# Two heads' scores of summed queries: 128 queries stationary, a PSUM bank for each head, and a new table of priorities

## The chip, the cores and the metric

The kernel runs on one core of one Trainium2 chip. The metric is the device time of one execution in microseconds (us). The kernel before took 773.06 us, the median of three runs that lie between 772.82 and 773.5 us. Instructions run on five engines: TensorE (PE in the profile), VectorE (DVE), ScalarE (ACT), GpSimd (POOL) and SyncE (SP), which here issues the DMAs.

## The reference

Three stages follow each other, all in float32.

- Attention over 4 batches, 8 heads, 576 positions of width 64, in two parts that are added. In the first, q, k and v are averaged over groups of four positions, which leaves 144 positions; softmax attention over these 144 gives an output that is repeated four times. In the second each position attends to the positions less than four away.
- A gated layer on 2304 tokens of width 512: `xk` and `xr` mix each token with the one before it, `k = relu(xk @ w_k)`, `v = k*k @ w_v` (1024 wide inside), `r = sigmoid(xr @ w_r)`, result `r * v`.
- A layer norm and a second pair of products, `x + relu(xn @ w_ch1) @ w_ch2`, 2048 wide inside.

```python
s = scale * np.matmul(qq, kk.transpose(0, 1, 3, 2))      # here 144 x 144 for each batch and head
s = s - np.max(s, axis=-1, keepdims=True)
a = np.exp(s)
a = a / (np.sum(a, axis=-1, keepdims=True) + 1e-09)
return np.matmul(a, vv)
```

## The kernel before, in words

The attention is cut into 16 units of one batch and two heads (`attention(n, ...)`). Head 0 lies on partitions 0 to 63, head 1 on 64 to 127. A unit loads q, k and v by DMA, brings q and k into a layout with the width on the partitions (`tq`, on TensorE, or a transpose on VectorE), sums groups of four (`qd`, `kd`), and computes the local scores (`sc`, two tiles of 48 small products and a mask) and the scores of the sums (`ds`). The softmax of `ds` takes a maximum (`mxd`, VectorE), a scaling by a small factor, and three exponentials on ScalarE (`pd`, one for each of three tiles of 144 columns). Then come transposes of `pd` (`tp`), the product with the summed v (`up`), the local product with v (`pv`), and the sum of the two into `xT`. With 144 queries in a head and 128 partitions, the kernel before computes three tiles: queries 0 to 63, 64 to 127 and 80 to 143 of both heads, each head on 64 output partitions. All three lie in one PSUM bank.

The second stage goes over 6 chunks of 384 tokens. For each chunk there are `psr` (36 products of 512 columns, `moe_r`), `psk` (96 of 384 columns, `moe_k`) and `psv` (72 of 512 columns, `accumulate`). Each product of two float32 matrices is written as three products of a high and a low part (`mm3`), which is why the names end in h and l. Weights come as raw words of 64 bits per element, are turned into float32 by ScalarE (lines 395 and 397) and VectorE (402 and 406), and are split into high and low parts (375, 376, 420). The third stage has `psh` and `pso` in the same manner.

What sets the order: every operation is first put on a list with an engine or a choice of engines, an estimated cost and a priority (`Plan.add`). `Plan.order` then goes through a model of the engines: among the operations that could start first, the one with the lowest priority number is taken, buffers are handed out in the order of their first use's priority, and short operations on TensorE (`thin`) may be kept together. The priorities come from the table `PRM` of some 150 numbers, so that any change of the table moves instructions on all engines. Each engine runs its own list in order; a waiting instruction holds all behind it. Where the model has TensorE idle, up to the moment at which the accumulators of the first chunk are handed out, the order is filled with products that nothing uses, line 433 (`warm`):

```python
if until.t is None:
    for _ in range(int((o.at - free) / fill_cost)):
        fill()
```

The PSUM has 8 banks: three for `pv0` to `pv2`, two in the ring `pk` (for `psr`, `psk`, `psh`) and three in the ring `pa`, from which all attention tiles of batches 1 to 3 are taken (line 445, `psa`). In batch 0, tiles are taken from a longer ring over all three groups.

Of the kernel before, what the change touches and what calls it, by code (L numbers as in the profile page):

```python
# [19 lines left out]
P = 128  # L20
# [4 lines left out]
    thin=89.915, t0=-16.294, t1=-9.875, t2=6.158, t3=7.667, t4=48.796, t5=19.99, t6=6.382, t7=-23.592, t8=-0.47,  # L25
    t9=-5.238, t10=-2.702, t11=0.12, t12=5.747, t13=-8.176, t14=-15.681, t15=-4.758, m0=2, m1=1, m2=0, m3=3, m4=1,
    m5=0, m6=0, m7=2, m8=3, m9=0, m10=0, m11=0, m12=0, m13=0, m14=0, m15=0, g0=0, g1=0, g2=0, g3=0, g4=0, g5=0, g6=0,
    g7=0, g8=0, g9=0, g10=0, g11=0, g12=0, g13=0, g14=0, g15=0, h0=1, h1=1, h2=1, h3=1, h4=0, h5=0, h6=0, h7=0, h8=0,
    h9=0, h10=0, h11=0, h12=0, h13=0, h14=0, h15=0, dve=0.27, pool=0, ta=-14.632, u0=4.274, tl=26.492, tm=4222.228,
    ld=33.163, ldv=76.41, mu=-14.605, wr=-0.059, wrs=-31.134, wka=-33.615, wkas=7.94, wkb=12.502, wkbs=-165.286,  # L30
    wv=103.601, wvs=2.875, wld=0.932, d0=235.165, d1=108.349, d2=260.708, d3=463.399, d4=581.694, d5=82886.056,
    a1=13.725, a1s=43.62, a1l=52.7, a2=-1.632, a2s=26.831, a2l=56.61, a3=54.215, a3s=40.382, a3l=96.628, xr=-60.685,
    xrs=16.307, xk=22.171, xks=1.12, xrn=9, xrns=1.512, xkn=-4.695, xkns=17.37, w2a=10.707, w2as=1.55, w2=7.281,
    w2s=34.846, wc=10.079, wcs=106.739, m2q=8, sld=-6.173, x1=3, wcg=-39.001, p0l=11.872, p0=2.352, p0s=3.263,
    p0n=7.723, dp=684.729, ra0=-8.097, ra1=-1.757, ra2=3.642, ra3=4.616, ra4=-5.44, ra5=0, rb0=0.342, rb1=19.209,
    rb2=16.653, rb3=33.463, rb4=10.116, rb5=0, rx0=-2.918, rx1=-13.421, rx2=8.601, rx3=12.062, rx4=-2.926, rx5=5.409,
    ne=12, we=52.842, wes=25.704, wel=6.378,
# [23 lines left out]
class Plan:  # L61
# [61 lines left out]
    def order(self):  # L123
# [17 lines left out]
        for k in sorted(range(nb), key=lambda k: first[k], reverse=True):  # L141
            turn[tag[k]].append(k)
# [123 lines left out]
def attn_moe_kernel(  # L266
# [186 lines left out]
    def attention(n, T0, TL):  # L453
# [194 lines left out]
        ds_ = psa(b, "ds")  # L648

        def dscore():  # L650
            if first:
                warm_up(2)
            for t, q0 in enumerate((0, 64, SD - 64)):
                for hp in range(2):
                    nc.tensor.matmul(
                        ds_()[64 * hp:64 * hp + 64, SD * t:SD * t + SD],
                        qd()[64 * hp:64 * hp + 64, q0:q0 + 64],
                        kd()[64 * hp:64 * hp + 64, :],
                        start=True, stop=True,
                    )  # L660
# [642 lines left out]
```

## Time and profile before

| | before |
|---|---|
| median of 3 runs | 773.06 us |
| the profiled execution | 771.95 us |
| its span, first to last instruction | 770.2 us |
| mean granted TensorE clock | 0.999 |
| TensorE busy | 753.6 us (98%) |
| VectorE busy | 524.6 us (68%) |
| ScalarE busy | 398.2 us (52%) |
| GpSimd busy | 63.8 us (8%) |

The profiled execution is one run with a profiler on; its span is 1.75 us shorter than its own time. "Busy" is the share in which at least one instruction was running on an engine. Matmuls overlap each other on TensorE, so that the step from one start to the next is the cost of a product, not its duration. One float32 product of the kernel in attention shows as two records (12 records of `ds` are 6 instructions).

### The profile page before, as it was taken

The page shows a single profiled execution, that of the slowest core. Times are in us where ns is not written, and L with a number is a line of the kernel's source. Part 1 is how long each engine was busy: PE and PEld are TensorE (multiplying, and loading weights), DVE is VectorE, ACT ScalarE, POOL GpSimd, SP SyncE. Part 2 cuts the span into 40 slices and gives each one's busy share as a digit, 9 for nine tenths or more (in the row PEclk, how much of TensorE's full clock was granted, in tenths as well). Part 3 has the DMA queues.
Part 4 walks back from the last instruction along what each step waited for, and adds up shares of the span by engine and source line. Part 5 has one row for each costly group of instructions (what it writes and reads, how often), then busy time and mean ns, then how long its engine had stood idle before and what let it go on. Part 6 is the DMA issues. An engine that isn't in the chain of part 4 may idle for free.

```text
span 770.2 us, 15665 instructions
## 1 busy us (share of the span) xinstructions
PE 753.6 (98%) x5816; PEld 650.2 (84%) x5816; DVE 524.6 (68%) x1083; ACT 398.2 (52%) x916; POOL 63.8 (8%) x113
## 2 busy tenths in 40 slices
PE   9999999999999999999999999999999999999997
PEld 6878787788788798888888888889889899889886
DVE  6899999998985959878889763486543364333233
ACT  6889997987884847868835431221421131111110
POOL 3101122112100000000110000020000020000000
PEclk9999999999999999999999999999999999999999
DMA  8997596867768895964689894379853347443322
GB/s 190 208 192 180 180 180 124 182 170 144 207 159 267 251 323 171 290 217 135 141 281 289 208 258 121 112 246 305 183 150 115 112 121 258 138 120 113 123 69 82
DMA packets 202854, 140.88 MB, mean 183 GB/s; under 512 B 127120, under 2 KB 160028, under 8 KB 202780
## 3 DMA queue, kind: packets, MB, share of 16 engines
q1 hardware_dynamic: 202780, 139.90, 66.6%
q8 instruction: 46, 0.75, 0.4%
q14 instruction: 28, 0.23, 0.1%
HBM read 107.88 MB, written 31.98 MB: 182 GB/s over the span
## 4 chain that ended last, share of the span: by engine, by line
PE 77%; DVE 10%; DMA 6%; ACT 4%; issue 2%; POOL 0%; SPq 0%; DVEq 0%; POOLq 0%; ACTq 0%
PE pso L779 8%; PE pso L778 8%; PE pso L780 8%; PE psh L778 7%; PE psh L779 7%; PE psh L780 7%; PE psk L778 4%; PE psv L778 4%; PE psk L780 3%; PE psk L779 3%; PE psv L779 3%; PE psv L780 3%; DMA w<-in_moe_w_ch_dram 3%; PE warm L433 2%; DVE tmu L802 1%
## 5 line engine op out<-in xcount | busy, mean ns | idle before, releaser
L778 PE MATMUL psh<-xn,sa 128*128 128x384 f32 x336 | 114.0, 339 | 2.4 <-DVE c L1114 1.2
L779 PE MATMUL psh<-xn,sa 128*128 128x384 f32 x336 | 113.6, 338 | 0.0
L780 PE MATMUL psh<-xn,sa 128*128 128x384 f32 x336 | 113.3, 337 | 0.0
L778 PEld LDWEIGHTS psh<-xn,sa 128*128 128x128 f32 x336 | 63.1, 188 | 11.0 <-DVE c L1114 2.1
L779 PEld LDWEIGHTS psh<-xn,sa 128*128 128x128 f32 x336 | 63.1, 188 | 6.1 <-DVE xn L1051 0.2
L780 PEld LDWEIGHTS psh<-xn,sa 128*128 128x128 f32 x336 | 63.1, 188 | 0.0
L379 ACT ACTIVATE c22h<-t 128x384 fp32r<-128x384 f32 x24 | 12.6, 525 | 83.7 <-DVE t L1106 78.6
L395 ACT ACTIVATE wf<-w 128x512 f32<-128x512 f32 x48 | 32.3, 673 | 17.4 <-DMA w<-in_moe_w_ch_dram 9.2
L402 DVE SCALAR_TENSOR_TENSOR wf<-wf,w 128x512 uint32<-128x512 uint32 x48 | 32.9, 687 | 11.1 <-ACT w L397 10.6
L379 ACT ACTIVATE kr<-psk 128x384 f32<-128x384 f32 x46 | 22.4, 488 | 25.2 <-PE psk L780 21.2
L379 ACT ACTIVATE c11h<-psh 128x384 fp32r<-128x384 f32 x23 | 11.3, 491 | 45.8 <-PE psh L780 45.7
L397 ACT ACTIVATE w<-w 128x512 uint32<-128x512 uint8 x52 | 35.0, 672 | 0.0
L843 DVE TENSOR_TENSOR kl<-kr,kh 128x384 fp32r<-128x384 f32 x43 | 23.8, 553 | 14.6 <-ACT kr L842 14.3
L1083 DVE SCALAR_TENSOR_TENSOR c11l<-psh,c11h 128x384 fp32r<-128x384 f32 x24 | 13.3, 554 | 29.1 <-ACT c11h L379 29.1
L802 DVE SCALAR_TENSOR_TENSOR tmu<-xT,oms,tmu 128x384 f32<-128x384 f32 (+1 forms) x64 | 31.7, 512 | 1.8 <-ACT tmu L796 1.8
L406 DVE SCALAR_TENSOR_TENSOR wf<-w,wf 128x512 uint32<-128x512 uint32 x48 | 32.7, 680 | 0.3
L1106 DVE TENSOR_TENSOR t<-psh,t 128x384 f32<-128x384 f32 x24 | 13.3, 554 | 28.5 <-PE psh L780 28.4
L1097 DVE TENSOR_TENSOR u<-psh,u 128x384 f32<-128x384 f32 x24 | 13.3, 555 | 27.2 <-PE psh L780 27.1
L379 ACT ACTIVATE c12h<-c 128x384 fp32r<-128x384 f32 x24 | 12.6, 525 | 37.0 <-DVE c L1110 36.9
L379 ACT ACTIVATE c21h<-c 128x384 fp32r<-128x384 f32 x24 | 12.6, 523 | 34.6 <-DVE c L1114 34.6
L796 ACT ACTIVATE tmu<-xT,vecs 128x384 f32<-128x384 f32 (+1 forms) x51 | 26.8, 539 | 6.9 <-DVE xrl L806 4.0
L1103 DVE TENSOR_TENSOR t<-psh,u 128x384 f32<-128x384 f32 x24 | 13.2, 552 | 20.2 <-PE psh L780 20.1
(527 smaller groups left out, 2164.5 us busy)
## 6 DMA issues: line engine op xcount, KB each, us to landing
sa<-s_dram SPq DMA_DIRECT2D x168, 256.0 KB, 2.7
w<-in_moe_w_ch_dram SPq DMA_DIRECT2D x32, 512.0 KB, 6.2
s_dram<-s SPq DMA_DIRECT2D x56, 256.0 KB, 4.0
vw<-in_v_dram SPq DMA_DIRECT2D x62, 96.0 KB, 4.0
x_dram<-r SPq DMA_DIRECT2D x18, 256.0 KB, 3.4
x1t<-x_dram SPq DMA_DIRECT2D x6, 768.0 KB
z_dram<-x1t SPq DMA_DIRECT2D x18, 256.0 KB, 2.7
zb<-z_dram SPq DMA_DIRECT2D x96, 48.0 KB, 2.8
```

Source lines behind the costliest of these rows:

```text
L379: return [("ACT", c_act(n, True), lambda: nc.scalar.activation(dst(), src(), AF.Relu), False), ("DVE", c_dve(n), lambda: nc.vector.tensor_ ...
L395: add("ACT", c_act(512), prio, lambda: nc.scalar.activation(f(), w64().bitcast(F32)[:, :, 1], AF.Abs, scale=2.0 ** -112), r=[w64], w=[f])
L397: add("ACT", c_act(512), prio, lambda: nc.scalar.activation(w64()[:, :, 0], w64().bitcast(U8).rearrange("p a (b c) -> p a b c", c=4)[:, :, ...
L402: lambda: nc.vector.scalar_tensor_tensor(fu(), fu(), 3, w64()[:, :, 0], op0=ALU.logical_shift_left, op1=ALU.bitwise_or),
L406: lambda: nc.vector.scalar_tensor_tensor(fu(), w64()[:, :, 1], 0x80000000, fu(), op0=ALU.bitwise_and, op1=ALU.bitwise_or),
L433: nc.tensor.matmul(warm()[:, :304], identb, isumb, start=True, stop=True)
L778: nc.tensor.matmul(ps, lh, rh, start=start, stop=False, skip_group_check=more)
L779: nc.tensor.matmul(ps, lh, rl, start=False, stop=False, skip_group_check=more)
L780: nc.tensor.matmul(ps, ll, rh, start=False, stop=stop, skip_group_check=more)
L796: add([("ACT", c_act(n, ap=1), lambda t=t, o=o, n=n, cur=cur, kt=kt: nc.scalar.mul(t()[:, o:o + n], cur(), mu[:, kt:kt + 1]), False), ("DV ...
L802: lambda t=t, o=o, n=n, prv=prv, kt=kt: nc.vector.scalar_tensor_tensor(t()[:, o:o + n], prv(), om[:, kt:kt + 1], t()[:, o:o + n], op0=ALU. ...
L843: add(either(C, lambda e: e.tensor_tensor(kl(), kr(), kh().bitcast(F32), op=ALU.subtract)), 0, prio, None, r=[kr, kh], w=[kl])
```

## The change

The scores of the sums are laid out anew. For each head one product takes queries 0 to 127 as the stationary operand, with 64 rows (the width) and 128 output partitions, and each head writes a bank of its own. The last 64 queries (80 to 143) of both heads follow as before, in the second 144 columns of the first bank. So there are four products in place of six, two banks in place of one, and two maxima on VectorE (over 288 and over 144 columns) in place of one over 432. The three exponentials read the same three tiles of 144 columns, in another arrangement of queries, and the transposes of `pd` write to correspondingly other columns. The planner's cost of the group goes from 1.0 to 0.65. Buffers whose first use has the same priority are now ordered by number, and nearly all numbers of `PRM` are replaced (two lines are shown).

```diff
-    thin=89.915, t0=-16.294, t1=-9.875, t2=6.158, t3=7.667, t4=48.796, t5=19.99, t6=6.382, t7=-23.592, t8=-0.47,
+    thin=86.006, t0=-18.938, t1=-10.122, t2=5.262, t3=7.862, t4=41.79, t5=17.974, t6=-4.597, t7=-24.316, t8=4.432,
...
-        for k in sorted(range(nb), key=lambda k: first[k], reverse=True):
+        for k in sorted(range(nb), key=lambda k: (first[k], k), reverse=True):
...
-        ds_ = psa(b, "ds")
+        ds_ = [psa(b, "ds") for _ in range(2)]
...
-            for t, q0 in enumerate((0, 64, SD - 64)):
-                for hp in range(2):
-                    nc.tensor.matmul(
-                        ds_()[64 * hp:64 * hp + 64, SD * t:SD * t + SD],
-                        qd()[64 * hp:64 * hp + 64, q0:q0 + 64],
-                        kd()[64 * hp:64 * hp + 64, :],
-                        start=True, stop=True,
-                    )
-
-        add("PE", 1.0 + hold(2), pr(0.3), dscore, r=[qd, kd], w=[ds_] + held, thin=True)
-        dsv = lambda: ds_()[:, :3 * SD].rearrange("p (t c) -> p t c", c=SD)
+            for hp in range(2):
+                nc.tensor.matmul(ds_[hp]()[:, :SD], qd()[64 * hp:64 * hp + 64, :P], kd()[64 * hp:64 * hp + 64, :],
+                                 start=True, stop=True)
+            for hp in range(2):
+                nc.tensor.matmul(ds_[0]()[64 * hp:64 * hp + 64, SD:2 * SD], qd()[64 * hp:64 * hp + 64, SD - 64:],
+                                 kd()[64 * hp:64 * hp + 64, :], start=True, stop=True)
+
+        add("PE", 0.65 + hold(2), pr(0.3), dscore, r=[qd, kd], w=ds_ + held, thin=True)
+
+        dsv = lambda: [ds_[0]()[:, :SD], ds_[0]()[:, SD:2 * SD], ds_[1]()[:, :SD]]
...
-        add("DVE", c_dve(432), pr(0.35),
-            lambda: nc.vector.tensor_reduce(mxd()[:, 0:3], dsv(), axis=AX.X, op=ALU.max), r=[ds_], w=[mxd])
+        add("DVE", c_dve(288), pr(0.35),
+            lambda: nc.vector.tensor_reduce(mxd()[:, 0:2], ds_[0]()[:, :2 * SD].rearrange("p (t c) -> p t c", c=SD),
+                                            axis=AX.X, op=ALU.max), r=[ds_[0]], w=[(mxd, 0)])
+        add("DVE", c_dve(144), pr(0.35),
+            lambda: nc.vector.tensor_reduce(mxd()[:, 2:3], ds_[1]()[:, :SD], axis=AX.X, op=ALU.max),
+            r=[ds_[1]], w=[(mxd, 2)])
...
-                lambda t=t: nc.scalar.activation(pd()[:, t], dsv()[:, t], AF.Exp, bias=mxd()[:, t:t + 1],
+                lambda t=t: nc.scalar.activation(pd()[:, t], dsv()[t], AF.Exp, bias=mxd()[:, t:t + 1],
...
-                r=[ds_, mxd], w=[(pd, t), (stat, 12 + t)])
+                r=[ds_[t // 2], mxd], w=[(pd, t), (stat, 12 + t)])
...
-                for t, q0 in enumerate((0, 64, SD - 64)):
-                    nc.tensor.transpose(tpv()[:, :, q0:q0 + 64], pd()[:, t, HS * kt:HS * kt + HS], ident)
+                for t, to in enumerate((tpv()[:, 0, :P], tpv()[:, :, SD - 64:], tpv()[:, 1, :P])):
+                    nc.tensor.transpose(to, pd()[:, t, HS * kt:HS * kt + HS], ident)
```

How the order changes is shown at three places. The first is TensorE in the first chunk of the second stage, right behind the first `psr` products, where the first `psk` products of the chunk stand (`xkh` and `xkl` are the chunk's tokens, `wk00h` to `wk30l` the weights of four blocks of 128 rows). Before, a group of `ds`, a second tile of `psk`, and five of the seven fill products that stand behind the first `psr`:

```order
L780 MATMUL psk<-xkh,wk20l 128x384
L655 MATMUL ds<-kd,qd 64x144 x6
L778 MATMUL psk<-xkh,wk00h 128x384
...
L780 MATMUL psk<-xkh,wk20l 128x384
L433 LDWEIGHTS identb
L433 MATMUL warm<-isum,identb 128x304
...
L778 MATMUL psk<-xkh,wk30h 128x384
```

Now, the same engine at the first group of `ds` in this chunk:

```order
L782 MATMUL psk<-xkh,wk30h 128x384
L783 MATMUL psk<-xkl,wk30h 128x384
L784 MATMUL psk<-xkh,wk30l 128x384
L655 MATMUL ds<-kd,qd 128x144 x2
L658 MATMUL ds<-kd,qd 64x144 x2
L782 MATMUL psk<-xkh,wk00h 128x384
```

The first two tiles of `psk` now run over all four blocks of weights before `ds`, and all fill products stand ahead of the first `psr`. Over the whole program, fill products go from 135 to 152: those ahead of the first `psr` from 128 to 152, those behind it from 7 to none. Changes between the wide products (`psr`, `psk`, `psv`, `psh`, `pso`) and anything else go from 93 to 105. One of the tiles of local scores (25 products) moves from ahead of the first `psr` to behind it. The split of the last block of `w_r` (`wr0l`, line 420) stays the 104th entry of VectorE's list, and its load the eighth load of a weight block in SyncE's.

The second place is TensorE at the border between the first and the second chunk. Before (`psv` with `wv7h` is the last of eight steps of an accumulator; `psv_1501` and `psv_1526` are its second and third accumulator):

```order
L780 MATMUL psr<-wr3h,xrl 128x512
L778 MATMUL psv_1501<-wv7h,kh 128x512
L779 MATMUL psv_1501<-wv7l,kh 128x512
L780 MATMUL psv_1501<-wv7h,kl 128x512
L778 MATMUL psr<-wr0h,xrh 128x512
...
L707 MATMUL tp<-isum,pd 72x2x64 x6
L778 MATMUL psv_1526<-wv7h,kh 128x512
L779 MATMUL psv_1526<-wv7l,kh 128x512
L780 MATMUL psv_1526<-wv7h,kl 128x512
L655 MATMUL ds<-kd,qd 64x144 x6
L718 MATMUL up<-pdT,vd 64x144 x4
L778 MATMUL psk<-xkh,wk00h 128x384
```

Now (the second and third accumulators are `psv_1459` and `psv_1469`):

```order
L782 MATMUL psv_1459<-wv7h,kh 128x512
L783 MATMUL psv_1459<-wv7l,kh 128x512
L784 MATMUL psv_1459<-wv7h,kl 128x512
L722 MATMUL up<-pdT,vd 64x144 x4
L752 MATMUL pv<-PT,vw 64x96 x12
L558 MATMUL tq<-isum,kin 128x120 x6
L782 MATMUL psv_1469<-wv7h,kh 128x512
L783 MATMUL psv_1469<-wv7l,kh 128x512
L784 MATMUL psv_1469<-wv7h,kl 128x512
L558 MATMUL tq<-isum,qin 128x120 x4
L782 MATMUL psr<-wr0h,xrh 128x512
```

All three accumulators of the first chunk are finished ahead of the first `psr` of the second, where two of them used to end between and behind its `psr` products.

The third place is VectorE in the first unit. Before:

```order
L640 TENSOR_REDUCE mx<-sc 128x6
L643 TENSOR_TENSOR e<-sc,mx 128x192
L420 TENSOR_TENSOR wr2l<-wf,wr2h 128x512
L667 TENSOR_REDUCE mxd<-ds 128x3
L677 TENSOR_REDUCE stat<-e 128x12
```

Now:

```order
L640 TENSOR_REDUCE mx<-sc 128x6
L667 TENSOR_REDUCE mxd<-ds 128x2
L420 TENSOR_TENSOR wr2l<-wf,wr2h 128x512
L643 TENSOR_TENSOR e<-sc,mx 128x192
L670 TENSOR_REDUCE mxd<-ds 128x1
L681 TENSOR_REDUCE stat<-e 128x12
```

The one maximum has become two, with other work between them.

## Rows read from the trace of the kernel before

**Rows 1.** The page's head: span, and TensorE's busy time.

```profile
span 770.2 us, 15665 instructions
...
PE 753.6 (98%) x5816; PEld 650.2 (84%) x5816; DVE 524.6 (68%) x1083; ACT 398.2 (52%) x916; POOL 63.8 (8%) x113
```

**Rows 2.** Windows: stretch, its length, then each engine's busy time (instructions).

```profile
2.00:57.30 55.30, 52.98 (x963) 41.27 (x961) 45.83 (x106) 41.66 (x117) 8.28 (x30) 1.00 1.03 203
57.30:240.00 182.70, 179.39 (x2310) 147.12 (x2301) 164.08 (x359) 153.65 (x396) 30.45 (x56) 1.00 0.73 171
240.00:460.00 220.00, 214.72 (x1044) 187.69 (x1043) 176.76 (x356) 138.85 (x279) 12.38 (x11) 1.00 0.80 238
```

**Rows 3.** Groups on TensorE: busy us, mean ns of one record, idle before.

```profile
L433 PE MATMUL warm<-isum,identb 128*128 128x304 bf16 x135 | 22.8, 308 | 2.0 <-DVE identb L326 1.8 <-issue 0.2
...
L655 PE MATMUL ds<-kd,qd 64*64 64x144 f32 x192 | 15.2, 291 | 0.0
```

**Rows 4.** Timeline around one `ds`: start us, duration us, engine, line, tiles, records.

```profile
161.68 0.33 PE L779 MATMUL psk<-xkl,wk31h 128*128 128x384 f32 x1
...
161.85 0.34 PE L780 MATMUL psk<-xkh,wk31l 128*128 128x384 f32 x1
...
162.12 0.95 PE L655 MATMUL ds<-kd,qd 64*64 64x144 f32 x12
...
163.00 1.21 PE L748 MATMUL pv<-PT,vw 128*64 128x96 f32 x24
...
164.14 0.50 PE L778 MATMUL psv<-wv2h,kh 128*128 128x512 f32 x1
...
164.47 0.39 PE L779 MATMUL psv<-wv2l,kh 128*128 128x512 f32 x1
```

**Rows 5.** Timeline of TensorE: fill products, full-height products, one tile of local scores.

```profile
25.77 2.24 PE L433 MATMUL warm<-isum,identb 128*128 128x304 bf16 x16
27.85 0.82 PE L707 MATMUL tp<-isum,pd 128*72 128x128 f32 x6
28.50 1.47 PE L604 MATMUL vs<-vw,wsum 128*72 128x128 f32 x12
29.91 0.72 PE L748 MATMUL pv<-PT,vw 128*64 128x96 f32 x12
...
72.27 0.25 PE L623 MATMUL sc<-maskb,identb 128*128 128x192 bf16 x1
...
72.99 0.26 PE L623 MATMUL sc<-maskb,identb 128*128 128x192 bf16 x1
```

**Rows 6.** Timeline ahead of the first `psr`, on ScalarE, VectorE and TensorE.

```profile
52.33 0.67 ACT L395 ACTIVATE wf<-w 128x512 f32<-128x512 f32 x1 [1.11 <-DMA w<-in_moe_w_r_dram]
...
56.93 0.92 DVE L420 TENSOR_TENSOR wr0l<-wf,wr0h 128x512 fp32r<-128x512 f32 x1
...
57.31 0.49 PE L778 MATMUL psr<-wr0h,xrh 128*128 128x512 f32 x1
```

**Rows 7.** Timeline at the second chunk: a store, ScalarE, TensorE.

```profile
136.81 1.86 SPq L863 DMA_DIRECT2D x_dram<-r  x1
...
142.45 0.60 ACT L822 ACTIVATE r<-psr 128x512 f32<-128x512 f32 x1 [1.70 <-DMA x_dram<-r]
...
143.10 0.44 PE L778 MATMUL psk<-xkh,wk00h 128*128 128x384 f32 x1 [1.48 <-ACT r L822]
```

**Rows 8.** Groups on VectorE: maxima over 192 and over 432 columns.

```profile
L640 DVE TENSOR_REDUCE mx<-sc 128x6 f32<-128x192 f32 x32 | 10.9, 346 | 1.0 <-PE sc L629 0.7
...
L667 DVE TENSOR_REDUCE mxd<-ds 128x3 f32<-128x432 f32 x16 | 9.5, 596 | 0.5 <-PE ds L655 0.4
```

**Rows 9.** Waits of TensorE for a PSUM tile's reader: total, times, longest (us).

```profile
PE tq L561 <- ACT ups L371: 1.0, 1, 1.0
...
PE tp L707 <- DVE xT L762: 0.4, 1, 0.4
```

**Rows 10.** Timeline: the last exponential that reads the `ds` of rows 4.

```profile
166.03 0.36 ACT L673 ACTIVATE pd<-ds,mxd 128x144 f32<-128x144 f32 x1
```

More of the change, by code (lines that the diff above doesn't have):

```diff
@@ L24 @@
 PRM = dict(
-    thin=89.915, t0=-16.294, t1=-9.875, t2=6.158, t3=7.667, t4=48.796, t5=19.99, t6=6.382, t7=-23.592, t8=-0.47,
-    t9=-5.238, t10=-2.702, t11=0.12, t12=5.747, t13=-8.176, t14=-15.681, t15=-4.758, m0=2, m1=1, m2=0, m3=3, m4=1,
+    thin=86.006, t0=-18.938, t1=-10.122, t2=5.262, t3=7.862, t4=41.79, t5=17.974, t6=-4.597, t7=-24.316, t8=4.432,
+    t9=-1.734, t10=4.242, t11=2.521, t12=0.116, t13=-10.093, t14=-4.939, t15=0.537, m0=2, m1=1, m2=0, m3=3, m4=1,
     m5=0, m6=0, m7=2, m8=3, m9=0, m10=0, m11=0, m12=0, m13=0, m14=0, m15=0, g0=0, g1=0, g2=0, g3=0, g4=0, g5=0, g6=0,
@@ L28 @@
     g7=0, g8=0, g9=0, g10=0, g11=0, g12=0, g13=0, g14=0, g15=0, h0=1, h1=1, h2=1, h3=1, h4=0, h5=0, h6=0, h7=0, h8=0,
[L29 to L37, printed above, removed]
+    h9=0, h10=0, h11=0, h12=0, h13=0, h14=0, h15=0, dve=0.286, pool=0, ta=13.998, u0=1.184, tl=23.071, tm=131.241,
@@ new lines @@
+    ld=38.056, ldv=129.431, mu=10.979, wr=6.876, wrs=-20.584, wka=-4.642, wkas=-2.051, wkb=14.259, wkbs=-32.139,
+    wv=113.112, wvs=3.386, wld=4.014, d0=203.946, d1=108.617, d2=425.731, d3=739.989, d4=1681.185, d5=5849569.365,
+    a1=5.837, a1s=41.207, a1l=48.778, a2=-1.89, a2s=26.385, a2l=49.833, a3=56.847, a3s=46.97, a3l=104.3, xr=-89.593,
+    xrs=22.848, xk=1.227, xks=5.399, xrn=9, xrns=0.867, xkn=-5.275, xkns=23.433, w2a=8.19, w2as=3.025, w2=-5.375,
+    w2s=47.665, wc=11.401, wcs=179.004, m2q=8, sld=-6.112, x1=3, wcg=-11.958, p0l=19.184, p0=-9.347, p0s=5.577,
@@ L38 @@
+    p0n=8.772, dp=762.448, ra0=9.241, ra1=-0.583, ra2=-20.548, ra3=-2.197, ra4=-6.884, ra5=0, rb0=-6.748, rb1=26.087,
+    rb2=3.111, rb3=48.319, rb4=-10.85, rb5=0, rx0=-4.413, rx1=-34.086, rx2=-4.413, rx3=-1.916, rx4=-4.961, rx5=2.524,
+    ne=12, we=98.705, wes=20.88, wel=3.677,
 )
```

## The prediction

> **What bounds the kernel now.** I read the page's head first: TensorE is busy for 753.6 of 770.2 us [rows 1], so the end can move only by what TensorE has to do and by the 16.6 us in which it does nothing. The windows say where those lie: 2.3 us between 2 and 57.3 us (the start, up to the first `psr`), 3.3 us between 57.3 and 240 us (attention of the later batches mixed with the second stage), 5.3 us between 240 and 460 us; the rest is before the first and behind the last product [rows 2]. From 460 us on there is none. VectorE is not the bound over the whole, but it has only 18.6 us to spare in the 182.7 us of the second window. TensorE's busy time is not all useful: 135 fill products hold 22.8 us, most of them at the start, and the `ds` groups 15.2 us [rows 3]. The profiled execution took 771.95 us, 1.1 us under the median of 773.06. Every term below is a difference against the profiled execution, and I put it on the median.
>
> **The products of `ds`.** One group before goes from 162.12 to 163.00 us: 0.88 us for 12 records [rows 4]. `psk` in front of it takes 0.27 us to the next start where its neighbour takes 0.17, and `psv` behind the thin group 0.33 to the next start [rows 4]: entering such a group costs TensorE about 0.1 us, and leaving it as much. The 12 records start in pairs, two heads at a time: 12 x 0.073. That they run together follows from products over the full height: 12 records of 128 columns take from 28.50 to 29.91 us, 0.117 each, and `ds` has 144 columns at 0.073 [rows 5, 4]. Now 8 records stand in place of 12. If the two heads with 128 output columns each run side by side as before, the group takes 8 x 0.073 = 0.59 us. The two kinds of product, 64 by 128 and 64 by 64, now stand next to each other, which the trace of before does not show; a switch of shape inside the group may cost what entering one does, 0.1 us, so 0.69 at the other end. I take 0.64, a saving of 0.24 us for a group. If they run one after the other, the first four records cost between 0.117 each and, scaled from 128 to 144 columns, 0.13; with 0.29 for the other four and 0.1 for the switch the group takes 0.86 to 0.91, so between 0.02 saved and 0.03 lost.
>
> The Trainium skill has a rule on this: TensorEngine Tiling (Array Packing), section Tiling Modes, says that changing the tiling mode, not just the tile, drains the engine. It speaks against the change, since a group now holds two modes. The 0.1 us on entering a group in rows 4 agrees with it in kind. By that rule alone a group takes 0.69 us, 16 groups save 0.8 us less than with my 0.64.
>
> **The fill products.** 16 of them take from 25.77 to 27.85 us, 0.13 each [rows 5]. Ahead of the first `psr` there are 24 more, +3.1 us; four `ds` groups there save 1.0; one tile of local scores leaves (72.27 to 72.99 us, 0.72 each [rows 5]). TensorE's own list ahead of the first `psr` is so 1.4 us longer. But TensorE stood idle for 2.3 us there [rows 2], waiting, and what the first `psr` needs last is the split of the last block of `w_r`: ScalarE, with all its list behind it, waits 1.1 us for the load, until 52.33, VectorE writes `wr0l` from 56.93, and `psr` starts at 57.31 [rows 6]. The order leaves that split and that load at the same place in their lists. So the fill takes the place of waiting. Bounds: 57.3 + 1.4 - 2.3 = 56.4 us if all waits vanish in it, 57.3 + 1.4 = 58.7 us if none does. I take 57.3, no change.
>
> **TensorE behind the first `psr`.** Seven fill products go: -0.9 us. The tile of local scores comes in: +0.7. Twelve groups of `ds` save 12 x 0.24 = 2.9. There are 12 more changes between wide products and others, at 0.1 us: +1.2. Sum -1.9 us (-2.5 with 0.59, -1.3 with 0.69, +0.8 with no saving). The transposes of `pd` keep their number and size, and I cost them at nothing, as only the columns that they write differ. Nothing hides them: all 96 lie on TensorE, so 0.01 us more or less for each would be 1 us.
>
> **The border of the chunks.** At 143.10 TensorE waits 1.48 us for ScalarE to empty a `psr` bank; ScalarE waits for a buffer `r`, and that for its store, issued at 136.81 and landed 5.6 us later [rows 7]. The store is late as the second accumulator of the first chunk ends among the `psr`. In the new order all accumulators end ahead of the `psr`, and 24 `psr` products with score tiles and a `ds` group stand between, some 8 us, against 0.7 for the multiplication, 5.6 for the store. I take the wait as gone: -1.5 us (bounds -1.5 and, if the loads ahead of the store on SP hold it longer, +1).
>
> **VectorE.** One maximum over 432 columns took 596 ns, one over 192 takes 346 [rows 8]: 1.04 ns a column and 146 ns fixed. 288 and 144 columns cost 446 + 296 = 742 ns, 0.15 more; 12 groups behind the first `psr` are 1.8 us more, against 18.6 us to spare [rows 2]. TensorE has other products to run meanwhile; if that cover is missing, all 1.8 us and the delay of other VectorE work come on top.
>
> **PSUM.** A `ds` group now holds two of the three banks of the ring, from its start at 162.12 to the last exponential at 166.03 [rows 4, 10], nearly 4 us in which scores, transposes, `up` and `pv` share one bank. TensorE waits for a reader of such tiles seldom now, 1.0 us at `tq` in the start and 0.4 at `tp` behind it [rows 9], the trace doesn't show it with two banks held. Bounds: 0, as the order puts `psk` and `psv`, which use other banks, between; and 0.4 us, the wait at `tp`, for each of the 12 units, 4.8 us. I take 1.0 us for PSUM and VectorE together, near the lower end, since the rows show so few waits.
>
> The Trainium skill says of it, TensorEngine Tiling (Array Packing), section Restrictions and Gotchas, that row tiling raises the pressure on PSUM because different row tiles must write to different banks. The second bank is that price; how long TensorE waits for it no row of before shows.
>
> **Sum.** 0 at the start, -1.9 behind it, -1.5 at the border, +1.0 for the new waits: -2.4 us, 773.06 - 2.4 = 770.7 us.
>
> **The rivals.**
> - *The start decides.* The fill products delay the first `psr` by their full 1.4 us, and 1.0 us is lost again at another border as the order is new everywhere: 773.06 - 2.4 + 2.4 = 773.1 us, no change. For it: TensorE is busy for 53 of the 55.3 us of the start [rows 2]. Against: the chain through the load of `w_r` [rows 6].
> - *Banks.* The two held banks cost 0.4 us a unit: 4.8 in place of 1.0, 773.06 - 2.4 + 3.8 = 774.5 us, slower. From 0.3 us a unit on (12 x 0.3 - 1.0 = 2.6) the whole gain is gone. For it: the hold of nearly 4 us, a quarter of the 15 us that a unit has between 57 and 240 us (182.7/12). Against: few such waits now [rows 9].
> - *The heads do not run side by side.* Nothing is saved in 12 groups, 2.9 us, and the start is 1.0 us longer at most: 773.06 - 2.4 + 2.9 + 0.5 = 774.1 us. Then the change doesn't do what it says. For it: no row of before has two products that differ only in the rows. Against: the pairs of `ds` run together in both rows and columns.
> - *More is gained.* The start ends at 56.4 us, and the new waits are 0: 773.06 - 2.4 - 0.9 - 1.0 = 768.8; with half of the 5.3 us between 240 and 460 us gone too [rows 2], 766.1.
>
> **How the numbers follow.** This kernel's measurements can tell about 0.2%, 1.5 us, from no change. Chances: my forecast 0.42, the start 0.20, banks 0.14, heads one after the other 0.10, more gained 0.14. The forecast's own range, 769.5 to 772.5 us, is faster for three quarters of it, 0.31, and unchanged for 0.11. Faster: 0.31 + 0.14 + 0.02 of the start = 0.47. Same: 0.11 + 0.15 of the start + 0.02 of the banks + 0.02 of the heads = 0.30. Slower: 0.03 + 0.12 + 0.08 = 0.23. The range, 767.0 to 775.0 us, leaves out the far half of the gains, and the worst of the banks.
>
> **What would show it.** `ds` in eight records that start in pairs over 0.6 to 0.7 us: right; 0.85 or more: the heads run in turn. The first `psr` near 57.3 us; no wait of 1.5 us at the first `psk` of the second chunk; waits of `sc`, `tp`, `up` or `pv` for exponentials in sum under 1 us more than now. TensorE's busy time should come out within 1 us of 753.6, since the fill products eat most of what `ds` saves. I am wrong if the first `psr` comes behind 58.5 us, if the idle time of TensorE between 57.3 and 240 us rises by over 2 us, or if the waits between 240 and 460 us change by as much, of which I say nothing: there the same products stand in almost the same order.

## The result, and the profile after

The change is slower: 779.91 us (median of 5 runs, 776.79 to 781.56) against 772.93 us for the kernel before (median of 5, 768.89 to 773.5), a ratio of 1.010 with a 95% interval of 1.007 to 1.013. I had forecast 770.7, and 775 as the upper end. The profiled execution took 779.81 us; its span is 7.8 us longer than in [rows 1].

The head of the page after, and the windows that answer to [rows 2] (stretch, length, TensorE's busy time and records, granted clock, DMA share, GB/s):

```profile
span 778.0 us, 15577 instructions
...
PE 760.1 (98%) x5769; PEld 651.0 (84%) x5769; DVE 527.6 (68%) x1096; ACT 394.9 (51%) x914; POOL 66.8 (9%) x118
```

```profile
2.00:57.30 55.30, 52.70 (x854) 1.00 0.98 191
57.30:240.00 182.70, 177.48 (x2299) 0.99 0.73 166
240.00:460.00 220.00, 215.29 (x1071) 1.00 0.80 235
```

TensorE is busy for 6.5 us more, and in the second window it is both less busy and at a clock that is not full. As the order is new, the windows don't hold the same work. I therefore compare by landmarks, the starts of products that both kernels have:

| us | before | after | grows by |
|---|---|---|---|
| first `tq` (behind the 24 opening fills) | 6.40 | 7.42 | 1.0 |
| from there to the first `psr` | 50.9 | 53.95 | 3.0 |
| first `psr` to the 37th (second chunk) | 69.7 | 74.1 | 4.4 |
| 37th `psr` to the first `psh` | 253.5 | 253.0 | -0.4 |
| first `psh` to the end | 389.7 | 389.6 | -0.2 |

The whole loss lies ahead of 136 us. The same kind of windows between the landmarks shows of what it is made: the start, the stretch from the first to the 37th `psr`, and the one from the 37th to the 109th (the second and third chunk); three rows of the kernel before, then three of the change.

```profile
6.40:57.31 50.91, 48.59 (x941) 1.00 1.04 195
57.31:126.99 69.68, 68.54 (x878) 1.00 0.72 169
126.99:253.34 126.35, 124.18 (x1502) 1.00 0.76 188
...
7.42:61.37 53.95, 50.47 (x900) 1.00 1.00 181
61.37:135.46 74.09, 70.28 (x808) 0.98 0.69 164
135.46:261.88 126.42, 125.89 (x1562) 1.00 0.77 184
```

In the start TensorE is busy for 1.9 us more and idle for 1.2 us more (3.48 in place of 2.32). In the second stretch it is idle for 2.7 us more, and busy for 1.7 us more at a lower clock. In the third it is idle for 1.6 us less and busy for 1.7 us more. There the first `psk` of the second chunk stands right behind the `psr`, without the wait of [rows 7]:

```profile
146.76 0.33 PE L782 MATMUL psk<-xkh,wk00h 128*128 128x384 f32 x1
```

Three places in the trace belong to the loss or to the expected gain.

**The group of `ds`.** A timeline of TensorE in the change; the row that begins at 13.94 is the second half of the first one, seen in a shorter stretch, and the last row is the product behind the group. Below it the weight loads of the four large records, as a group (minimum, median and maximum in ns):

```profile
13.71 0.52 PE L655 MATMUL ds<-kd,qd 64*128 64x144 f32 x4
...
13.94 0.29 PE L655 MATMUL ds<-kd,qd 64*128 64x144 f32 x2
...
14.16 0.46 PE L658 MATMUL ds<-kd,qd 64*64 64x144 f32 x4
14.55 0.71 PE L561 MATMUL tq<-isum,kin 96*128 96x96 f32 x6
...
L655 PEld LDWEIGHTS ds<-kd,qd x64: 182/184/187, 13.7 to 231.3; 64*128 64x128 f32 x64
```

The group takes 0.84 us; before, it took 0.88 [rows 4]. The two heads do run side by side (their starts are 6 ns apart), but the pairs follow each other after 0.23, 0.22 and 0.17 us. In the kernel before, only the first of the six pairs took 0.17, the others 0.12. The same view of the kernel before has its weight loads:

```profile
L655 PEld LDWEIGHTS ds<-kd,qd x192: 129/133/133, 12.7 to 221.1; 64*64 64x64 f32 x192
```

**The wait near 90 us.** Timeline of the change on TensorE, VectorE and ScalarE (in brackets the idle time ahead and what ended it), then the windows behind it:

```profile
89.92 0.48 PE L655 MATMUL ds<-kd,qd 64*128 64x144 f32 x2 [2.57 <-DVE e L643]
90.60 0.51 PE L655 MATMUL ds<-kd,qd 64*128 64x144 f32 x2 [0.20 <-ACT pdT L715]
...
93.08 0.63 PE L784 MATMUL psv<-wv2h,kl 128*128 128x512 f32 x1
93.51 0.63 PE L782 MATMUL psv<-wv2h,kh 128*128 128x512 f32 x1
...
88.83 0.68 DVE L402 SCALAR_TENSOR_TENSOR wf<-wf,w 128x512 uint32<-128x512 uint32 x1
89.43 0.34 DVE L643 TENSOR_TENSOR e<-sc,mx 128x192 f32<-128x192 f32 x1
...
87.14 0.67 ACT L395 ACTIVATE wf<-w 128x512 f32<-128x512 f32 x1 [1.66 <-DMA w<-in_moe_w_k_dram]
```

```profile
87.50:90.00 2.50, 0.08 (x1) 1.00 0.04 10
90.00:92.50 2.50, 2.30 (x17) 0.92 0.56 200
92.50:95.00 2.50, 2.50 (x8) 0.50 0.78 247
95.00:97.50 2.50, 2.50 (x21) 0.89 0.92 201
```

To be read from below: ScalarE waits for a block of `w_k`; VectorE's conversion of that block stands ahead of `e`, which empties a bank of the ring `pa`; and `ds`, which now needs two of the three banks, waits for it 2.57 us and for the second bank, which `pdT` empties on ScalarE, 0.20 more. Behind the wait the granted clock is 0.50, the lower level of 1.2 GHz, for a whole slice of 2.5 us: `psv` starts come 0.43 us apart (93.08 and 93.51) in place of 0.23. Over the three slices from 90 us, (0.08 + 0.50 + 0.11) x 2.5 = 1.7 us of full clock are missing, so TensorE ran for some 3.4 us at the lower level. These 1.7 us and the 2.7 us of idle time make up the 4.4 us by which this stretch grew.

**The start.** Timeline of the change on TensorE, SyncE and ScalarE, answering to [rows 5, 6]:

```profile
29.00 1.50 PE L604 MATMUL vs<-vw,wsum 128*72 128x128 f32 x12 [1.45 <-DMA vw<-in_v_dram]
...
58.41 0.55 PE L561 MATMUL tq<-isum,qin 96*128 96x96 f32 x4 [0.88 <-ACT ups L371]
...
61.37 0.50 PE L782 MATMUL psr<-wr0h,xrh 128*128 128x512 f32 x1
...
50.26 0.42 SPq L389 DMA_DIRECT2D w<-in_moe_w_r_dram  x1
...
54.53 0.70 ACT L395 ACTIVATE wf<-w 128x512 f32<-128x512 f32 x1 [0.41 <-DMA w<-in_moe_w_r_dram]
```

The load of `w_r` is issued at 50.26, where the kernel before issued it at 45.61, and ScalarE has it 2.2 us later than in [rows 6]. The row of the kernel before:

```profile
45.61 1.71 SPq L389 DMA_DIRECT2D w<-in_moe_w_r_dram  x1
```

### The profile page after: what moved, and what is told of

Read it like the earlier page. It is cut to its first block, busy times and chain, and to the rows that moved or that the text cites. A ratio compares the mean times of both kernels' runs of the same rounds, so it can differ in the third digit from the quotient of the medians.

```text
span 778.0 us, 15577 instructions
## 1 busy us (share of the span) xinstructions
PE 760.1 (98%) x5769; PEld 651.0 (84%) x5769; DVE 527.6 (68%) x1096; ACT 394.9 (51%) x914; POOL 66.8 (9%) x118
## 4 chain that ended last, share of the span: by engine, by line
PE 77%; DMA 8%; DVE 7%; ACT 6%; issue 1%; SPq 1%; POOL 0%; DVEq 0%; ACTq 0%; POOLq 0%
PE pso L783 8%; PE pso L782 8%; PE pso L784 8%; PE psh L782 7%; PE psh L783 7%; PE psh L784 7%; PE psk L782 4%; PE psk L784 4%; PE psk L783 4%; PE psv L782 3%; PE psv L783 3%; PE psv L784 3%; PE warm L433 2%; DMA w<-in_moe_w_k_dram 2%; PE pv L752 2%
## 5 line engine op out<-in xcount | busy, mean ns | idle before, releaser
L782 PEld LDWEIGHTS psh<-xn,sa 128*128 128x128 f32 x336 | 63.1, 188 | 10.6 <-DVE c L1118 1.7
L800 ACT ACTIVATE tmu<-xT,vecs 128x192 f32<-128x192 f32 (+1 forms) x52 | 26.4, 526 | 4.2 <-DVE xrl L810 1.4
L433 PE MATMUL warm<-isum,identb 128*128 128x304 bf16 x152 | 26.2, 315 | 1.8 <-DVE identb L326 1.8
```

The lines of the kernel that those rows point to most:

```text
L433: nc.tensor.matmul(warm()[:, :304], identb, isumb, start=True, stop=True)
L782: nc.tensor.matmul(ps, lh, rh, start=start, stop=False, skip_group_check=more)
L800: add([("ACT", c_act(n, ap=1), lambda t=t, o=o, n=n, cur=cur, kt=kt: nc.scalar.mul(t()[:, o:o + n], cur(), mu[:, kt:kt + 1]), False), ("DV ...
```

## The experiments

`layout_only` and `table_only` have orders of their own, `before_again` and `before_wait` that of the kernel before, all others that of the change, apart from what the edit moves. "Start" is from the first `tq` to the first `psr`, "stretch" from there to the 37th, both in the profiled execution; the ratio is to runs of the kernel before on the same chip.

| kernel | us (runs) | ratio [95%] | start | stretch | waits of TensorE near 90 us |
|---|---|---|---|---|---|
| before | 772.93 (5) | 1 | 50.9 | 69.7 | 0.34 |
| after | 779.91 (5) | 1.0100 [1.0068, 1.0132] | 53.95 | 74.1 | 2.57, 0.20 |
| layout_only | 778.83 (6) | 1.0087 [1.0059, 1.0115] | 54.2 | 72.6 | 0.43 |
| table_only | 785.83 (6) | 1.0172 [1.0144, 1.0199] | 52.7 | 71.2 | |
| e_first | 779.33 (6) | 1.0089 [1.0064, 1.0114] | 55.7 | 72.8 | 2.29 |
| fill128 | 777.88 (8) | 1.0073 [1.0048, 1.0099] | 54.8 | 73.2 | 2.62 |
| e_pdT_first | 777.36 (9) | 1.0061 [1.0039, 1.0084] | 53.5 | 72.4 | 1.46, 0.23 |
| fill_vs | 778.60 (10) | 1.0084 [1.0056, 1.0111] | 55.6 | 72.6 | 2.34 |
| combined | 778.27 (10) | 1.0078 [1.0055, 1.0101] | 55.1 | 72.5 | 1.46 |
| ds72 | 778.71 (1) | | 55.0 | 72.8 | 2.67 |
| banks_wv2 | 778.85 (5) | 1.0098 [1.0071, 1.0125] | 57.2 | 71.3 | 0.23, 1.79 |
| start_acts | 778.31 (6) | 1.0094 [1.0069, 1.0120] | 53.3 | 73.5 | 2.62 |
| lists | 778.47 (6) | 1.0098 [1.0069, 1.0126] | 55.2 | 73.7 | 0.48, 0.23, 1.77 |
| before_again | 771.42 (1) | | 50.5 | 71.4 | 0.34 |
| after_again | 779.96 (1) | | 54.4 | 73.8 | 2.72 |
| before_wait | 773.78 (12) | 1.0031 [1.0013, 1.0050] | 50.85 | 73.4 | 2.04 |

**layout_only and table_only.** The change's code with the old `PRM`, and the old layout with the new `PRM` (both with the new order of buffers of equal priority).

```diff
-    thin=86.006, t0=-18.938, ...
+    thin=89.915, t0=-16.294, ...
```

> The new layout of ds (two banks, two maxima, four products) and the new tie-break, with the old table of priorities; the planner orders all anew. Theory 1 (the layout itself costs, as its order of the start has more fill products and its ds waits for a bank): 777 to 780 us, a first psr at 60 to 61 us, and a wait of ds for a reader of a bank of over 1 us somewhere between 60 and 130 us. Rival (the new table costs, the layout nothing): 772 to 774 us and a first psr at 57 to 58 us.

> The old layout of ds (one bank, one maximum, six products) with the new table of priorities and the new tie-break. Theory 1 (the layout costs): 772 to 775 us, a first psr within 1 us of 57.3 us, no wait of ds for a bank over 0.5 us. Rival (the table costs): 778 to 780 us.

Each half alone is slower than the kernel before, and the table with the old layout is slower than the whole change. So no part of the change is a gain that the other part spoils; each of the three new orders loses, and at different places. `layout_only` has the time and the first `psr` (60.9 us) of its theory 1, but no wait of `ds` between 60 and 130 us: its two long waits, 2.2 us at 29.20 and 2.0 at 220.09, stand elsewhere, and the clock falls behind both (lowest slices 0.50 and 0.57). `table_only` is slower than either of its theories. It loses behind 380 us: TensorE waits 2.46 us at 389.98 and 1.56 at 392.81, and from 392.5 to 402.5 us the granted clock is 0.53. The new order of buffers of equal priority is in both kernels; no run tests it alone.

**e_first.** For the one unit whose `ds` waits, VectorE's `e` stands right behind its maximum.

```diff
+        late, early = self.pull
+        seq.remove(late)
+        seq.insert(seq.index(early) + 1, late)
```

> The changed kernel with its order held fixed but for one instruction: VectorE's subtraction e (line 643) of the second score tile of the sixth unit, which frees the bank that ds waits 2.57 us for at 89.92 us, stands right behind the maximum mx of that tile instead of six entries later, behind the conversion of weights that waits for a load. Theory 1 (two banks for ds make TensorE wait for that reader, and the idle time then halves TensorE's granted clock from about 92 to 96 us): the wait goes to under 0.5 us, the clock stays at 1.00 there, and the time falls by 2.6 + 1.5 to 2 us, to about 775.5 us. Rival (ds waits for the next thing as long, or VectorE's later work gives it back): within 1 us of 779.9 us.

TensorE in `e_first` (its lines lie a few further down):

```profile
88.50 0.51 PE L660 MATMUL ds<-kd,qd 64*128 64x144 f32 x2
91.30 0.51 PE L660 MATMUL ds<-kd,qd 64*128 64x144 f32 x2 [2.29 <-ACT pdT L720]
```

The first head's product starts without a wait; the second waits for its bank nearly as long as both did before (2.29 us in place of 2.57 and 0.20). The wait for `e` was one of two, and the time stays at 779.3 us, as the rival has it.

**fill128 and fill_vs.** 24 fill products fewer, taken evenly from the first 96; and the 18 left out that stand ahead of `tp`, `pv` and `ds` behind the late `vs`.

```diff
+                        self.n_fill += 1
+                        if self.n_fill % 4 or self.n_fill > 96:
+                            fill()
```

```diff
-                if until.t is None:
+                if until.t is None and i not in (112, 118, 207):
```

> The changed kernel with its order held fixed but for 24 fill products left out ahead of the first psr (128 in place of 152, every fourth of the first 96). Theory 1 (the fill lies on TensorE's path to the first psr): first psr earlier by 2.5 to 3.2 us, at 58 to 59 us, time 777 us. Rival (the fill takes the place of waiting, as predicted): first psr within 0.7 us of 61.4 us, time 779 to 780 us. A third way: the clock falls where fill is missing, and the time rises.

> The changed kernel in its own order without the 18 fill products that stand, between the sum of v of the second unit (it came 1.45 us late, at 29.00) and the ds group at 43.35, ahead of tp, pv and ds. Theory (fill products behind a late operand lie on the path of the start): the keys' transposes of the next unit (tq) start at about 34.7 in place of 36.52, ds at 41.0 in place of 43.35, the first psr 2 us earlier, at 59.3, and the time is 777.9 against 779.9. Rival (other engines set the start, the fill stands in place of waiting): the gaps become waits for ScalarE and loads, the first psr stays within 0.7 us of 61.4, and the time stays at 779 to 780 or gets worse where the granted clock falls.

In neither does the first `psr` come earlier. In `fill128` it starts at 61.77, where the rival had it; the wait for `vs` behind the left-out products is 2.78 us, and the clock falls behind it to 0.50 (30.0 to 32.5 us), the third way of the expectation. Its time of 777.88 us lies between theory and rival. TensorE in `fill_vs`, and its windows at the end of the start:

```profile
32.89 0.72 PE L752 MATMUL pv<-PT,vw 128*64 128x96 f32 x12 [1.03 <-ACT PT L375]
...
58.75 0.90 PE L561 MATMUL tq<-isum,qin 96*128 96x96 f32 x4 [1.24 <-ACT ups L371]
59.44 2.49 PE L433 MATMUL warm<-isum,identb 128*128 128x304 bf16 x9
```

```profile
57.50:60.00 2.50, 1.26 (x8) 0.72 1.12 178
60.00:62.50 2.50, 2.50 (x14) 0.59 1.21 188
```

The next transposes (`tq`) start at 36.51, as before the edit (36.52), though 14 of the 18 fills stood ahead of them: a wait for `PT` is there instead. The rival of `fill_vs` is right in kind. Its start is even longer, as the clock falls behind the wait for `ups`, and nine fill products take 2.49 us. As the clock fell in both profiles, they don't show what fewer fill products would be worth without that.

**e_pdT_first, and combined with fill_vs.** Now both readers are moved: besides `e`, ScalarE's two copies `pdT` stand ahead of the conversion that waits for its load.

```diff
+        for i in self.pdt:
+            seq.remove(i)
+        at = max([seq.index(wf)] + [seq.index(i) + 1 for i in self.tps])
+        seq[at:at] = self.pdt
```

> The changed kernel in its own order, but for one unit (the one whose ds waited 2.57 us at 89.92) both readers that empty the score ring are moved forward: VectorE's subtraction for the second head's local scores stands right behind its maximum, and ScalarE's two copies of the transposed weights stand ahead of the conversion of w_k that waits for its load. In e_first, where only the first was moved, the second bank took the place of the first (wait 2.29 us). Theory (the two banks of a ds group, each emptied by an engine that stands behind the same late load of w_k, make the wait, and the clock falls after it): ds starts at about 88.2 without a wait over 0.5 us, the granted clock stays at 1.00 from 90 to 97.5 us, and what lies behind comes 3 to 4 us earlier, 776.4 us against 779.9. Rival (the work behind ds is late by the same load anyway): another wait of 2 us or more stands within 10 us behind it, and the time stays at 779 to 780.

> Both edits together: readers of the ring moved forward for the one unit, and the 18 fill products left out. If the two losses are apart and both theories hold: 779.9 - 3.5 - 2.0 = 774.4 us, near the kernel before (773.4). If only the banks count 776.4, if only the fill 777.9, if neither 779.9.

TensorE in `e_pdT_first`, and its windows:

```profile
85.46 0.75 PE L671 MATMUL ds<-kd,qd 64*128 64x144 f32 x4
...
88.70 0.50 PE L801 MATMUL psv<-wv2h,kh 128*128 128x512 f32 x1 [1.46 <-ACT wv2h L388]
```

```profile
87.50:90.00 2.50, 1.08 (x3) 1.00 0.54 154
90.00:92.50 2.50, 2.50 (x17) 0.64 0.66 225
92.50:95.00 2.50, 2.50 (x12) 0.68 0.99 251
```

The wait of `ds` is gone, so the two banks and the engines that empty them did make it. But 1.46 us come back right behind the group, at `psv`, the clock falls there as well, and of the 4.4 us that the stretch had grown 1.7 come back. Its ratio is the lowest of the change's variants, yet the intervals overlap. `combined` adds nothing to it.

**banks_wv2, start_acts, lists.** The conversion of `wv2` ahead of the copies `PT`, on top of `e_pdT_first`; in the start, ScalarE's conversions of the first `w_v` behind its cast `wr0h`; and both.

```diff
+        after(wv2 + 5, wv2 + 4, wk01 + 1)
...
+        after(wv0 + 2, wr0 + 5)
+        after(wv0 + 1, wr0 + 5)
```

> As e_pdT_first (both readers of the score ring forward, for the unit whose ds waited 2.57 us). There the wait of ds was gone, but the next product behind it, psv, waited 1.46 us for ScalarE to write wv2h, and the granted clock still fell to 0.64 and 0.68 between 90 and 95 us. Here wv2h and wv2l are written earlier too: ScalarE and VectorE convert wv2 ahead of their copies of PT. Theory (the clock falls because TensorE stands still there; without the wait it stays): no wait over 0.5 us between 80 and 100 us, clock 1.00 there, and from the first psr to the 37th (72.4 us in e_pdT_first, 74.1 in the change, 69.7 before) 69.5 to 70.5 us; the time is 2 us under e_pdT_first, about 775.4 us. Rival (the work behind the late load is late whatever the order): the next wait is for PT, w_k or v, as long as before, and the stretch stays at 72 to 73 us.

> The changed kernel in its own order, but in the start ScalarE's two conversions of the first w_v block stand behind its cast of wr0h; in the change ScalarE waits 0.65 us for that load at 57.52 with the copy ups and wr0h queued behind it, and TensorE waits 0.88 us for ups. Theory (the split of wr0 and ups behind this load set the end of the start): no wait at tq for ups, the first psr 1.0 us earlier counted from the first tq, 52.9 to 53.0 us in place of 53.95, and the time 1 us under the change. Rival (13 fill products, scores and the other preparations of psr end there anyway): the first psr stays within 0.4 us of 53.95 behind the first tq, and the time is the change's.

> The edits of banks_wv2 and start_acts together. If both theories hold, the two places give back 4.5 + 1.0 us: 774.4 us against 779.9 of the change, and within 2 us of the kernel before on this chip; if only the first holds 775.4, if neither 778 to 780. What is then left against the kernel before is the longer start, about 2 us.

In `banks_wv2` TensorE runs from 85 to 92 us with one wait of 0.23 us, and then waits again. TensorE, and ScalarE ahead of it:

```profile
94.43 0.72 PE L788 MATMUL pv<-PT,vw 128*64 128x96 f32 x12 [1.79 <-ACT ups L398]
...
93.60 0.60 ACT L402 CAST wk01h<-wf 128x512 fp32r<-128x512 f32 x1
94.11 0.27 ACT L398 COPY ups<-up 128x144 f32<-128x144 f32 x1
```

From 88.35 to 94.38 ScalarE has 0.18 us of idle time: what TensorE needs next is at the end of a full list, in each of the orders tried. That is the rival in kind: the work behind the late load stays late. In this profile the clock stays at 1.00 behind the 1.79 us, and the stretch is 71.3 us, within the 69.7 to 71.4 of the kernel before's two profiles. `lists` has the same edits there and nearly the same wait (1.77 us), but the clock falls to 0.50 behind it, and the stretch is 73.7. So most of the difference between these two, 1.7 of 2.4 us, is whether the clock falls. The time of `banks_wv2` is no better; in its profile the start took 57.2 us, with the clock at 0.81 and 0.51 from 57.5 to 62.5. `start_acts` removes the wait at `tq` for `ups`; two of 0.26 and 0.18 us at `sc` take its place. Its start is 0.66 us under that of `after`, where the theory had 1.0, but only 0.2 under that of `e_pdT_first`, whose start has no edit; the times show nothing. `lists` is no better than either.

**ds72.** The first pair of each group over 72 columns in place of 144.

```diff
-                nc.tensor.matmul(ds_[hp]()[:, :SD], qd()[64 * hp:64 * hp + 64, :P], kd()[64 * hp:64 * hp + 64, :],
+                nc.tensor.matmul(ds_[hp]()[:, 72:SD], qd()[64 * hp:64 * hp + 64, :P], kd()[64 * hp:64 * hp + 64, 72:],
```

> The first pair of each ds group (two heads, 128 queries) runs over 72 of its 144 columns, in the same order otherwise; half of these queries' scores are left out, and the other half stands in their place. Theory (the load of 128 weight columns sets the step of the pair): the two starts stay 0.20 to 0.22 us apart and the group takes 0.80 us or more in place of 0.84. Rival (the columns set it, as they do for the 64 by 64 products at 0.125 us): the starts come 0.11 to 0.13 us apart and the group takes 0.62 to 0.66. Time about 779.5 by the first, 16 x 0.2 = 3 us less by the second.

TensorE in `ds72`:

```profile
13.76 0.45 PE L655 MATMUL ds<-kd,qd 64*128 64x72 f32 x4
14.14 0.46 PE L658 MATMUL ds<-kd,qd 64*64 64x144 f32 x4
14.53 0.71 PE L561 MATMUL tq<-isum,kin 96*128 96x96 f32 x6
```

Neither: the group takes 0.77 us, the first step is 0.167 us in place of 0.227. 72 columns fewer take 0.060 off, so in this step the columns count in full (144 of them 0.12, the step of the later pairs before); 0.107 remains that doesn't depend on them. At the switch of shape they take only 0.01 off (0.21 in place of 0.22). For the first pair of 64 by 64 the same sum leaves 0.174 - 0.120 = 0.054. The difference of the two, 0.053, is that of the weight loads, 184 - 132 = 52 ns (132 is the median of the 64 by 64 loads in the change). So I read it as a weight load that isn't hidden behind the first pair after a change of shape; no run here changes the load alone.

**before_again, after_again.** Both kernels unchanged, profiled a second time.

> The kernel before, unchanged, profiled once more, for how far one execution's start differs from another's. If the longer start is the change's, the first psr comes 50.5 to 52.0 us behind the first tq, as in the first profile (50.9), and the granted clock is 1.00 up to there. If starts differ as much by themselves, it comes behind 53 us.

> The change, unchanged, profiled once more: the first psr 53.5 to 57.2 us behind the first tq, as in the five profiles that share its start (53.95, 55.66, 53.5, 55.0, 57.2), the wait of ds near 90 us between 2.3 and 2.7 us.

Both as expected, but for the wait of `ds`, which is 2.72 us, just above its range: the starts of the kernel before lie within 0.4 us (50.5 to 50.9, `before_wait` among them), and none of the change's is under 53.3. The longer start belongs to the change. Its stretch is 2.4 to 4.4 us longer, as that of the kernel before differs by 1.7 between its two profiles.

**before_wait.** The kernel before, with one instruction of VectorE four places later; all others stand as they did.

```diff
+        dve.remove(late)
+        dve.insert(dve.index(at) + 1, late)
```

> The kernel before, in its own order but for one VectorE instruction: wk01l (1.0 us) is written behind the next four on VectorE's list (qT, ups, qd, the conversion of wv3), so that psk, which waits 0.34 us for it at 88.70, waits about 2.5 us. Theory (one wait of such a length costs its length and then the clock's fall behind it, as in the change, where 2.57 us of waiting was followed by 2.5 us at 0.50): granted clock under 0.8 in some 2.5 to 5 us behind the wait, and the 37th psr comes 3.5 to 4.2 us later counted from the first, 73.2 to 73.9 us in place of 69.7; the time is 0.4 to 0.5% up. Rival (the wait costs its own length alone): clock 1.00 throughout, the 37th psr 2.2 us later, 0.3% up. Third: later waits vanish in it and the time hardly moves.

TensorE in `before_wait`, and its windows:

```profile
92.14 0.69 PE L798 MATMUL psk<-xkh,wk01l 128*128 128x384 f32 x1 [2.04 <-DVE wk01l L438]
92.63 0.52 PE L796 MATMUL psk<-xkh,wk11h 128*128 128x384 f32 x1
92.95 0.52 PE L797 MATMUL psk<-xkl,wk11h 128*128 128x384 f32 x1
```

```profile
90.00:92.50 2.50, 0.46 (x2) 0.91 0.58 187
92.50:95.00 2.50, 2.50 (x17) 0.50 0.00 0
95.00:97.50 2.50, 2.50 (x13) 0.91 0.49 112
```

The wait grew by 1.7 us, from 0.34. The clock falls to 0.50 behind it, and `psk` starts come 0.32 us apart where they came 0.17. From the first `psk` to the 37th `psr` TensorE now takes 64.6 us, against 61.0 and 61.9 in the two profiles of the kernel before: 2.7 to 3.6 us for 1.7 of waiting. The whole is 0.31% slower, 2.4 us. The theory's 0.4 to 0.5% lies at the edge of the interval, and the rival's 0.3% fits as well, so the time alone doesn't decide between them; the clock does. It fell in the profile, and all 12 runs have a mean granted clock of 0.996 to 0.998, where 45 of the 63 runs of the kernel before that stand beside the experiments have 0.999 or 1.000.

## Why the prediction was wrong, point by point

- **The products of `ds`: the size of the term was wrong.** "If the two heads with 128 output columns each run side by side as before, the group takes 8 x 0.073": they run side by side, and the group takes 0.84 us. I carried the mean step of a long row of equal pairs to a group of two unequal ones. Each of the two has the long first step, and the switch between them takes 0.22 from start to start. 0.04 us are saved for a group where I had 0.24: 0.5 us in place of 2.9 behind the first `psr`. Not even that arrives as a whole. Counted from the first start of a group to the start behind it, without idle time, the twelve groups take 10.8 and 10.3 us in the two profiles of the change against 10.6 before: seven or eight of them take 0.84, the others up to 1.31 (the one at 89.92). And the sum's "+0.8 with no saving" should be +1.0 (-0.9 + 0.7 + 1.2). The Trainium skill, TensorEngine Tiling (Array Packing), section Tiling Modes, says that changing the tiling mode drains TensorE; the trace agrees only in part, with 0.22 at the switch against 0.12 between the later pairs of one mode, since the first step within a mode is as long or nearly so, 0.23 and 0.17, without a switch.
- **The fill products: half right.** That they stand in place of waiting held in the main: leaving out 24 or 18 of them made no start shorter, though the clock fell in both profiles. That waiting would shrink by as much did not hold: it grew by 1.2 us, and TensorE's work by 1.9. "I take 57.3, no change" failed by 4.1 us, outside my bounds. 1.0 of it is ahead of the first `tq`, where the same 24 products took 5.71 us in place of 4.69 (4.55 to 6.01 over all profiles, of either kernel). That is the clock: the trace's record of it shows full speed from 4.71 us on in the kernel before and from 6.78 on in the change, and the products start 0.25 us apart up to there and 0.13 behind. In the three profiles of the kernel before's order it rises at 4.71, 5.75 and 6.72 us, so this 1.0 is luck of the execution. 3.0 are the change's. I had reasoned that the split of `w_r` and its load keep their places in the lists. They do; but a place in a list is no time. Other loads that wait stand ahead of it, and the load went out 4.65 us later. Nor does that split hold the first `psr`: in [rows 6] the product starts at 57.31, without a wait, while `wr0l` is still being written. What TensorE last waits for ahead of it is `ups`, 1.0 us [rows 9] and 0.88 in the change. ScalarE writes `ups` right behind the conversion of a load that it waits for, of `w_r` before (52.33), of `w_v` in the change (57.52). I found no single cause of the 3.0 us: no fill edit shortens it, and the one wait at its end that I removed gave 0.66 at most, within the spread of the starts.
- **PSUM: the mechanism of the rival, in another shape.** I spread 0.3 to 0.4 us over twelve units. In fact the list of waits has 0.7 us for eleven of them together (`tp` 0.4, `pv` 0.3), and 2.77 for one. A wait that arises where a second bank, a late load and two in-order lists meet isn't a small tax on every unit.
- **The clock: left out.** Behind that wait TensorE ran some 3.4 us at half its clock, which cost 1.7 us. No term of mine had a price for a wait beyond its length; `before_wait` shows that there is one.
- **The border of the chunks: right, but it doesn't show in the landmarks.** The first `psk` of the second chunk starts at 146.76, right behind its `psr`, without the 1.48 us of [rows 7]. From the 37th `psr` to the 109th it is 126.4 us in both kernels all the same. TensorE is idle there for 1.6 us less and busy for 1.7 us more, as scores have moved there from ahead: the records of `sc` in that window go from 694 to 784 and their busy time from 10.9 to 12.5 us, while the two windows ahead have 49 fewer each. So the gain came, and the loss in the two windows ahead is larger than their growth shows, by the scores that left them.
- **VectorE: right.** The two maxima take 448 and 292 ns, where I had 446 and 296.

What stands against 7.0 us: 3 to 4 of a longer start, 2.4 to 4.4 from the first to the 37th `psr`, with the wait and the clock behind it, and from 136 us on nothing that goes beyond the spread of the profiles. That the wait causes the second part is shown in kind by `before_wait`, and by the sum of idle time and clock. It isn't shown as a time that can be got back, since each repair of a list left the next wait. The cause of the longer start stays open. No version tried is faster than the kernel before.

The mean granted clock of the runs bounds what the clock can explain. The five of the change have 0.991 to 0.998, and the profiled one has the highest, so the others lost more clock than its trace shows, at places that no profile shows. But one run each of `start_acts` and `lists` has 1.000, and they took 777.39 and 776.97 us, some 6 us above the 770.76 of the kernel before on that chip. So in these two variants of the change most of the loss is there without a fall of the clock.

## What to carry to other kernels

When a change lets a planner set the whole order anew, the order is the change: price it by where late loads meet the in-order lists, not by the instructions saved. Take the step of a product from the place in a group at which it stands, first or later, and not from the group's mean. And ask of every new wait of TensorE what the clock will be behind it.

## What the runs showed of the hardware that I had not expected

- Waits of TensorE of 1.46 to 2.7 us were followed by a granted clock of 0.50 to 0.64 in the lowest of the 2.5 us slices behind them (`after`, `e_pdT_first`, `start_acts`, `before_wait`). One of 1.79 us in `banks_wv2` was not, nor one of 2.47 at 28.86 us in the same profile, and one of 1.77 in `lists` was (0.50). So the length alone doesn't say whether the clock falls.
- A weight load of 64 rows by 128 columns takes 184 ns, one of 64 by 64 takes 132. The first step behind a change of shape is longer by as much, 0.227 us against 0.174; that the load makes this difference is argued from `ds72`, not shown.
- The same 24 products at the opening took from 4.55 to 6.01 us, without a difference in the code ahead of them, as the granted clock rose to full speed at 4.41 us in one profile (`banks_wv2`) and at 7.42 in another (`fill_vs`).
